# A convolution and a token mixer on one core: chunks enter the rounds three at a time, and the first step's sums lie in other buffers

## The chip, the cores and the metric

The kernel runs on one core of a Trainium2 chip. The metric is the device time of one execution in microseconds; the time before is the median of three runs.

## The reference

The input `x` is 8 x 4224 x 192 (batch, token, channel). A causal convolution with 7 taps per head runs over the tokens; the taps are a softmax of `weight`. Its result, again called `x`, goes through a phase mixer:

```
x     = conv(x, softmax(weight))              # 8 heads of 24 channels, 7 taps
theta = x @ w_theta                           # 192 x 192
zr, zi = x * cos(theta), x * sin(theta)
y     = w_tok_r @ zr + w_tok_i @ zi           # over the 4224 tokens, both matrices 4224 x 4224
u     = x + y
out   = u + relu(u @ w_ch)                    # 192 x 192
```

Nearly all of the arithmetic is the two token products.

## The kernel before

**Chunks, blocks and steps.** The 4224 tokens that are summed over are cut into 33 chunks of 128 (`NK`), the 4224 output tokens into 33 blocks of 128. Two blocks form a unit, so there are 17 units (`NU`), the last with one block only. A chunk is prepared once: its convolved `x`, its cosine and sine products and some differences of them lie in a tile `z` of seven fields. It then stays for 17 consecutive steps, and in each step it meets one unit. Eleven chunks (`NW`) fit at a time: the pool `zpool` has eleven slots. The list `base` says in which step of a round each of the eleven enters, and `start` extends it to three rounds of 18 steps; a slot so has one step between two chunks. A step `t` thus works on `n` chunks (2 to 11) and one unit. There are 58 steps.

**A step's products.** The four products of a two-block unit with real and imaginary weights are done with seven runs instead of eight (sums of weights and of `z` fields, as in Strassen's scheme). A run takes each of the `n` chunks in turn, with a pair of matmuls per chunk (`L405`, 128 x 384, two halves of the columns). A unit of one block takes four runs. The results stand in PSUM tiles `y`, two of them (`ypool`); `give` adds a finished one to the sums `pv` in SBUF on VectorE (`L370`), or, in the first 17 steps, copies some of them on ScalarE (`L368`). A tile `y` is used again only after the `give` that reads it. At the end of a step the sums go to `part` in device memory (`L418`) and come back 17 steps later (`L341`); in the last 17 steps they are final, `x` is added (`add_x`), and `outputs` casts, transposes, multiplies by `w_ch` and stores them.

**Weights.** For each step, pieces of the two token matrices are loaded by POOL's queue to `st` (`L295`), two steps ahead. VectorE turns them to `wt` (`L308`, four turns) and forms four sums of weights (`L320`), one step ahead.

**Chunks.** `load_chunk` loads a window of the input, `xw`, in four pieces by POOL's queue (`L183`); four halo pieces are copied from the window of the chunk before by SP's queue (`L174`). The preparation is a list of tasks: two `conv` (eight matmuls each at `L196`, copied out by ScalarE at `L148`; after the second, the convolved rows are stored to `xs`, `L213`), two `transpose` (`L153`), two `theta` (`L138`, with two sines on ScalarE at `L233`), two `product` (`L238`) and two `sums` (`L244`) on VectorE. All matmul results but `y` share a PSUM pool of two buffers (`mmpool`).

**Buffers.** Windows `xw` and sums `pv` share the tag `big` of the pool `wk`, with six slots.

**Order.** The helpers `pe`, `dve`, `act` and `pool` keep the written order on four engines (POOL's for weight loads and `add_x`, not for windows). Inside a step, work is put among the mix pairs at times counted in sevenths of the step: `step_events` gives a time to each task, `mix` carries it out when that point comes. The tasks of chunks that enter in the next step stand at 0.1 plus 0 to 3.6, and the next chunk's 2.3 later.

**The fill.** The first eleven chunks are prepared by the loop at `L611`, one conv-to-sums pipeline over 13 iterations. `between(n)` puts up to `n` mix pairs between the stages, as far as their chunk is `ready` (chunk `i-2` from the middle of iteration `i`); in the iterations 1 and 2 matmuls on a zero tile (`idle`, `L537`, here called noise) fill in.

Of the kernel before, what the change touches and what calls it, by code (L numbers as in the profile page):

```python
# [12 lines left out]
F32 = mybir.dt.float32  # L13
# [3 lines left out]
def kernel(  # L17
# [27 lines left out]
    P = nc.NUM_PARTITIONS  # L45
    assert (B, D, P) == (8, 192, 128) and S % P == 0
    N = B * D
# [13 lines left out]
    NW = 11  # L61
    PC = 512

    base = [0, 0, 1, 1, 2, 3, 3, 4, 4, 5, 5]
    assert len(base) == NW
    start = [base[k % NW] + (NU + 1) * (k // NW) for k in range(NK)]
    NSTEP = start[-1] + NU
# [26 lines left out]
    wk = ctx.enter_context(tc.tile_pool(name="wk", bufs=2))  # L94
    zpool = ctx.enter_context(tc.tile_pool(name="zpool", bufs=NW))
# [64 lines left out]
    Z11, T1, Z21, Z22, T2, T4, T3 = range(7)  # L160
# [102 lines left out]
    def load_chunk(k):  # L263
        if k < NK and k not in chunks:
            chunks[k] = Chunk(k, before=chunks[k - 1] if k % NW else None)
# [7 lines left out]
    class Step:  # L273
# [62 lines left out]

        def load_rows(self):
            for tb in self.tbs:
                pv = wk.tile([P, N], F32, name="pv", tag="big", bufs=6)
                if not self.first:  # L340
                    nc.sync.dma_start(  # L341
                        out=pv, in_=part[(self.t // NU - 1) % 2][tb, :, :]
                    )
                self.pv.append(pv)
# [122 lines left out]
    def step_events(t):  # L467
        found = []
        s = steps[t]
        if t + 1 < NSTEP:  # L470
            found += steps[t + 1].w_tasks()
            found.append((1.6, steps[t + 1].load_rows))
            if steps[t + 1].final and not steps[t + 1].ahead:
                for i in range(len(steps[t + 1].tbs)):
                    found.append((3.3 + 1.7 * i, lambda i=i: steps[t + 1].add_x(i)))
        for s in steps[t:]:
            if s.ahead and t == s.t - (4 if s.late else 10):
                for i in range(len(s.tbs)):
                    found.append((3.3 + 1.7 * i, lambda s=s, i=i: s.add_x(i)))
        if t + 2 < NSTEP:  # L480
            nxt = steps[t + 2]
            for m in (1, 2):
                found.append((1.3 + 3 * (m - 1), lambda m=m: nxt.load_w(m)))
        for at, f in outputs:
            begin = at - sum(s.time for s in steps[:t])
            if 0 <= begin < steps[t].time:
                found.append((7 * begin / steps[t].time, f))
        if t >= NU - 2:
            new = [k for k in range(NK) if start[k] == t + 2 and k >= NW]
            for k in new:  # L490
                found.append((4.5, lambda k=k: load_chunk(k)))
            at = 0.1
            for k in (k for k in range(NK) if start[k] == t + 1 and k >= NW):
                pos = [0, .5, 1.3, 1.6, 2.1, 2.5, 3.1, 3.15, 3.4, 3.6]

                def add(at, j, k):
                    def go():
                        if j == 0:
                            chunks[k].todo = chunks[k].tasks()
                        next(chunks[k].todo)()  # L500
                    found.append((at, go))
                for j, p in enumerate(pos):
                    add(at + p, j, k)
                at += 2.3
        return found


# [10 lines left out]
    for a in range(2):  # L518
        nc.gpsimd.affine_select(
            out=sel, in_=sel, pattern=[[1, Q - 1 + 2 * WR]], channel_multiplier=-1,  # L520
            base=-(Q - 1 + HALO - KS + 1 + a * WR), compare_op=ALU.not_equal, fill=1.0,
# [13 lines left out]
    def idle(n):  # L535
        for _ in range(n):
            pe(nc.tensor.matmul(  # L537
                spare[:, 0, 0:BH], lhsT=noise[:, 0:P], rhs=noise, start=True, stop=True
            ))
# [47 lines left out]
    def stream():  # L587
        for t in range(NSTEP):
            yield from steps[t].mix(step_events(t))
# [5 lines left out]
    def more(n):  # L595

        for i in range(n):
            if need[0] is None:
                need[0] = next(flow, NK)
            if need[0] > ready[0]:  # L600
                return n - i
            need[0] = next(flow, NK)
        return 0
# [7 lines left out]
    for i in range(NW + 2):  # L611
        ch = chunks.get(i) if i < NW else None
        old = chunks[i - 1] if 0 < i <= NW else None

        def between(n):
            left = more(n)
            if 0 < i < 3:
                idle(min(left, 2))

        if ch:  # L620
            ch.conv(0)
        between(3)
        if old:
            old.theta(0)
        between(2)
        if ch:
            ch.conv(1)
        if i == 0:
            idle(4)
        ready[0] = i - 2  # L630
        between(3)
        if old:
            old.theta(1)
        if i == 1:
            for _, f in steps[0].w_tasks():
                f()
        if i + 3 < NW:
            load_chunk(i + 3)
        between(2)
        if ch:  # L640
            ch.transpose(0)
        if old:
            old.product(Z11)
        between(1)
        if ch:
            ch.transpose(1)
        between(1)
        if old:
            old.product(Z21)
            old.sums(0)  # L650
            old.sums(1)
        between(2)
    nc.vector.memset(wch[:, 1:3, :], 0.0)
    for rows, i, part_w in channel_pieces(moe_w_ch):
        nc.gpsimd.dma_start(out=wch[rows, i, :], in_=part_w)
# [34 lines left out]
```

## Time and profile before

| what | value |
|---|---|
| median of 3 runs | 1474.13 us (1471.6 to 1476.81) |
| the profiled execution's own time | 1474.01 us |
| its span in the profile | 1472.3 us |
| TensorE (PE) busy | 1435.7 us, 10100 matmuls |
| VectorE (DVE), ScalarE (ACT) busy | 1001.1 us, 361.1 us |
| mix matmuls (L405) | 7656 |
| matmuls on the zero tile (L537) | 36 |
| stores of sums to `part`, loads back | 79 and 79, 768 KB each |
| windows of the input, pieces (L183) | 132 |

In the profile a row names line, engine and operation, then what is written and read, and how often. PE is the matmul, PEld the weight load, DVE is VectorE, ACT ScalarE, POOL GpSimd and SP SyncE. In a timeline a line begins with start and duration in us; brackets at the end hold the idle time of the engine before it and what ended it. Matmuls overlap, so the duration of one is longer than its distance to the next.

### The profile page before, as it was taken

What the parts mean: (1) busy time and instruction counts of PE and PEld (TensorE: products, weight loads), DVE (VectorE), ACT (ScalarE), POOL (GpSimd) and SP (SyncE); (2) the same over time, 40 slices, a digit from 0 to 9 for tenths busy, and PEclk for the clock granted to TensorE, in tenths of its full rate; (3) what the DMA queues carried; (4) which work ended last, traced back from release to release, by engine and by line L of the source; (5) the groups of instructions that cost most, each with busy time, mean ns of one, the idle gap of its engine ahead of it and who ended that gap; (6) DMA issues with size and microseconds to landing.
All of it is one profiled execution on the core that took longest, in us unless ns stands there. A gap on an engine that the chain in (4) does not pass through costs nothing.

```text
span 1472.3 us, 24451 instructions
## 1 busy us (share of the span) xinstructions
PE 1435.7 (98%) x10100; PEld 905.6 (62%) x10100; DVE 1001.1 (68%) x1050; ACT 361.1 (25%) x461; POOL 429.4 (29%) x659
## 2 busy tenths in 40 slices
PE   7899999999999999999999999999999999999997
PEld 5565666666666666566666656666666666666664
DVE  6784545454548687766666657778787778778585
ACT  5771111111134254000000005245122222222234
POOL 7422211121233232211112323332224243544220
PEclk9999999999999999999999999999999999999999
DMA  9986657465699999987779989999778777999873
GB/s 165 201 187 145 130 98 152 95 145 102 120 246 218 214 243 241 202 215 152 215 154 224 226 184 231 191 229 263 144 176 200 190 177 180 211 253 223 198 200 109
DMA packets 234975, 274.16 MB, mean 186 GB/s; under 512 B 69104, under 2 KB 202608, under 8 KB 234864
## 3 DMA queue, kind: packets, MB, share of 16 engines
q0 software_dynamic: 163616, 95.30, 49.1%
q1 hardware_dynamic: 71248, 177.30, 33.9%
q8 instruction: 79, 1.29, 0.3%
q14 instruction: 32, 0.26, 0.1%
HBM read 245.49 MB, written 111.28 MB: 242 GB/s over the span
## 4 chain that ended last, share of the span: by engine, by line
PE 87%; DMA 5%; DVE 4%; ACT 1%; issue 1%; SPq 0%; POOL 0%; DVEq 0%; ACTq 0%; POOLq 0%
PE y L405 78%; PE v L138 5%; PE tp L153 2%; PE pc L196 2%; DVE pv L370 1%; DVE wt L308 1%; DMA part<-pv 1%; DMA xw<-xw 1%; DMA st<-in_moe_w_tok_i_dram 1%; DVE z L244 1%; DMA xw<-in_x_dram 1%; ACT z L233 1%; DVE z L238 1%; DMA pv<-part 1%; DVE pv L434 0%
## 5 line engine op out<-in xcount | busy, mean ns | idle before, releaser
L405 PE MATMUL y<-z,wt 128*128 128x384 f16 x7656 | 1297.6, 326 | 12.4 <-DVE pv L370 11.6
L405 PEld LDWEIGHTS <-wt 128*128 128x128 f16 x7656 | 738.4, 98 | 481.6 <-issue 17.5
L370 DVE TENSOR_TENSOR pv<-y,pv 128x768 f32<-128x768 f32 x324 | 308.6, 953 | 376.2 <-PE y L405 362.9
L308 DVE STREAM_TRANSPOSE wt<-st 128x1408 f16<-128x1408 f16 (+7 forms) x224 | 326.5, 1463 | 4.8 <-DMA st<-in_moe_w_tok_i_dram 4.6
L295 POOL DMA_DIRECT2D st<-in_moe_w_tok_i_dram x232 | 132.5, 579 | 502.9 <-DVE wt L308 487.6
L295 POOL DMA_DIRECT2D st<-in_moe_w_tok_r_dram x232 | 132.5, 579 | 467.1 <-DVE wt L308 447.8
L320 DVE TENSOR_TENSOR wt<-wt 128x1408 f16<-128x1408 f16 (+7 forms) x216 | 204.0, 945 | 10.9 <-PE y L405 8.2
L148 ACT ACTIVATE uT<-tp 128x768 f16<-128x768 f16 x127 | 102.2, 814 | 294.9 <-PE tp L153 293.3
L148 ACT ACTIVATE z<-pc 128x768 f16<-128x768 f32 x65 | 52.9, 813 | 387.0 <-PE pc L196 387.0
L368 ACT ACTIVATE pv<-y 128x768 f32<-128x768 f32 x66 | 53.6, 815 | 280.1 <-PE y L405 279.8
L138 PEld LDWEIGHTS <-uT 128*128 128x128 f16 x1056 | 91.8, 98 | 24.0 <-issue 8.3
L434 DVE SCALAR_TENSOR_TENSOR pv<-v,pv 128x768 f32<-128x768 f32 x66 | 62.6, 950 | 44.3 <-PE v L138 42.1
L183 POOL DMA_DIRECT2D xw<-in_x_dram x132 | 76.1, 584 | 28.3 <-DMA st<-in_moe_w_tok_r_dram 9.8
L424 ACT ACTIVATE ub<-pv 128x768 f16<-128x768 f32 x66 | 54.8, 837 | 90.2 <-DVE pv L370 89.2
L244 DVE TENSOR_TENSOR z<-z 128x768 f16<-128x768 f16 x132 | 73.5, 557 | 4.2
L233 ACT ACTIVATE z<-v,half_pi 128x768 f16<-128x768 f32 x66 | 59.5, 902 | 45.9 <-PE v L138 45.9
L238 DVE TENSOR_TENSOR z<-z 128x1536 f16<-128x1536 f16 x66 | 60.6, 949 | 13.4 <-ACT z L233 13.4
L352 POOL TENSOR_TENSOR pv<-pv,xr 128x1536 f32<-128x1536 f32 x20 | 62.5, 3124 | 7.6 <-issue 6.9
L138 PE MATMUL v<-wch,uT 128*128 128x192 f16 x528 | 54.2, 246 | 3.9 <-DVE pv L434 2.2
L138 PE MATMUL v<-wth,uT 128*128 128x192 f16 x528 | 55.3, 248 | 1.4 <-ACT z L233 1.3
L233 ACT ACTIVATE z<-v 128x768 f16<-128x768 f32 x66 | 53.1, 805 | 0.0
L153 PE MATMUL tp<-ident,z 128*128 128x128 f16 x396 | 33.4, 222 | 6.3 <-ACT z L233 6.2
(43 smaller groups left out, 203.0 us busy)
## 6 DMA issues: line engine op xcount, KB each, us to landing
part<-pv SPq DMA_DIRECT2D x79, 768.0 KB, 4.1
pv<-part SPq DMA_DIRECT2D x79, 768.0 KB, 5.4
out_dram<-pv SPq DMA_DIRECT2D x66, 384.0 KB, 4.4
st<-in_moe_w_tok_r_dram POOLq DMA_DIRECT2D x136, 176.0 KB, 6.0
st<-in_moe_w_tok_i_dram POOLq DMA_DIRECT2D x136, 176.0 KB, 4.8
xs<-z SPq DMA_DIRECT2D x132, 96.0 KB, 4.3
xw<-in_x_dram POOLq DMA_DIRECT2D x121, 96.0 KB, 5.8
part<-xs POOLq DMA_DIRECT2D x26, 384.0 KB, 6.9
```

The costliest lines, as they stand in the source:

```text
L138: pe(nc.tensor.matmul(v[:, k, b * D : (b + 1) * D], lhsT=tT[:, 3 * k + b + i, :], rhs=w[:, 2 * b + i, :], start=(i == 0), stop=(i == 1),))
L148: act(nc.scalar.activation(out=out, in_=in_, func=AT.Copy))
L153: pe(nc.tensor.transpose(tp[:, 0, k * P : (k + 1) * P], u[:, k * P : (k + 1) * P], ident))
L183: nc.gpsimd.dma_start(out=self.xw[lo : lo + n, h, :, :], in_=x[:, t0 : t0 + n, :].rearrange("b s d -> s b d"),)
L233: act(nc.scalar.activation(**args))
L238: dve(nc.vector.tensor_tensor(out=o, in0=xv, in1=o, op=ALU.mult))
L244: dve(nc.vector.tensor_tensor(out=z[:, o, :], in0=z[:, a, :], in1=z[:, b, :], op=ALU.subtract))
L295: pool(nc.gpsimd.dma_start(out=st[a * Q : (a + 1) * Q, 0:nb, :, 0:n] .rearrange("i r bt s -> i (r bt) s"), in_=w[self.tbs[0] * P : (self.t ...
L308: dve(nc.vector.transpose(self.w[name][:, 0 : self.n, :, :], self.st[int(name[1])][:, int(name[0]) - 1, :, 0 : self.n * Q] .rearrange("p b ...
L320: dve(nc.vector.tensor_tensor(out=self.w[name][:, 0 : self.n, :, :], in0=self.w[a][:, 0 : self.n, :, :], in1=self.w[b][:, 0 : self.n, :, : ...
L370: dve(nc.vector.tensor_tensor(out=o, in0=yv, in1=o, op=ALU.add))
L405: pe(nc.tensor.matmul(y[cn][:, q, 0:BH], lhsT=self.w[wn][:, c, :, :].rearrange("p bt i -> p (bt i)"), rhs=chunks[k].z[:, zn, q * BH : (q + ...
```

## The change

Four things change. The list `base` lets three chunks enter per step instead of mostly two, which makes 56 steps of 58; the steps at the seams hold 3, 6, 9 and 8 chunks where they held 2, 4, 5, 7, 9 and 10, and the last steps 8, 5 and 2 where they held 9, 7, 6, 4 and 2. The sums of step 0 are taken from `zpool`, whose slots the later chunks use, and not from `big`. In later rounds the tasks of the next entering chunk start 1.6 instead of 2.3 after those of the one before. In the fill the calls of `between` allow 10 pairs an iteration instead of 14, and stand between the two `sums` too.

```diff
-    base = [0, 0, 1, 1, 2, 3, 3, 4, 4, 5, 5]
+    base = [0, 0, 0, 1, 1, 1, 2, 2, 2, 3, 3]
...
             for tb in self.tbs:
-                pv = wk.tile([P, N], F32, name="pv", tag="big", bufs=6)
+                if self.t == 0:
+                    pv = zpool.tile([P, N], F32, name="pv", tag="z")
+                else:
+                    pv = wk.tile([P, N], F32, name="pv", tag="big", bufs=6)
...
                 for j, p in enumerate(pos):
                     add(at + p, j, k)
-                at += 2.3
+                at += 1.6
...
         if ch:
             ch.conv(0)
-        between(3)
+        between(2)
         if old:
             old.theta(0)
-        between(2)
+        between(1)
         if ch:
             ch.conv(1)
         if i == 0:
             idle(4)
         ready[0] = i - 2
-        between(3)
+        between(2)
         if old:
             old.theta(1)
...
         if i + 3 < NW:
             load_chunk(i + 3)
-        between(2)
+        between(1)
         if ch:
             ch.transpose(0)
         if old:
@@
         between(1)
         if ch:
             ch.transpose(1)
+        if old:
+            old.product(Z21)
         between(1)
         if old:
-            old.product(Z21)
             old.sums(0)
+        between(1)
+        if old:
             old.sums(1)
-        between(2)
+        between(1)
```

## The prediction

> **What bounds the kernel now.** First the page: busy shares, the 40 slices, the chain that ended last, the costliest group.
>
> ```profile
> PE 1435.7 (98%) x10100; PEld 905.6 (62%) x10100; DVE 1001.1 (68%) x1050; ACT 361.1 (25%) x461; POOL 429.4 (29%) x659
> ...
> PE   7899999999999999999999999999999999999997
> ...
> PE 87%; DMA 5%; DVE 4%; ACT 1%; issue 1%; SPq 0%; POOL 0%; DVEq 0%; ACTq 0%; POOLq 0%
> ...
> L405 PE MATMUL y<-z,wt 128*128 128x384 f16 x7656 | 1297.6, 326 | 12.4 <-DVE pv L370 11.6
> ```
>
> TensorE is the bound: 98% busy, full in all slices but the first two and the last. The change keeps all 7656 mix matmuls and every chunk's own work, so it moves the time only through TensorE's idle time. Where is that? The stage table (us, then busy of PE, weight load, DVE, ACT, POOL; clock; DMA share; GB/s) and TensorE's timeline say:
>
> ```profile
> 50.80:92.62 41.82, 38.13 (x350) 25.07 (x350) 36.26 (x52) 36.12 (x49) 17.63 (x31) 1.00 1.13 234
> 92.62:113.04 20.42, 16.75 (x136) 11.16 (x136) 19.01 (x27) 12.22 (x16) 5.21 (x9) 0.98 0.60 116
> ...
> 453.80:480.50 26.70, 26.70 (x217) 17.16 (x216) 22.39 (x27) 12.68 (x16) 6.82 (x12) 1.00 1.03 249
> ```
> ```profile
> 42.40 0.80 PE L405 MATMUL y<-z,wt 128*128 128x384 f16 x2 [3.89 <-DVE pv L370]
> 42.99 1.48 PE L138 MATMUL v<-wth,uT 128*128 128x192 f16 x8
> ...
> 96.97 0.82 PE L138 MATMUL v<-wth,uT 128*128 128x192 f16 x8
> ...
> 99.48 0.49 PE L153 MATMUL tp<-ident,z 128*128 128x128 f16 x6 [0.38 <-ACT z L233]
> ...
> 113.04 12.18 PE L405 MATMUL y<-z,wt 128*128 128x384 f16 x66 [3.29 <-DVE pv L370]
> ```
>
> Idle sits in the fill (0 to 113 us, with two waits above 3 us for a sum, "give", that stood late in VectorE's queue) and in the tail after 1440. In the seams where later chunks enter (427 to 587, 878 to 1034) it is 0.73, 0.41, 0.73, 0.48 and 0.80: 3.15 us in all. A step there (third row) is full on TensorE, with VectorE at 22.4 of 26.7 us.
>
> **What the Trainium skill says.** "TensorE: Matmul & The Clock Gate" (Part 1) lets the clock fall to half after an idle window of about 3.4 us. The trace agrees: after 3.89 us idle, eight theta matmuls took 1.48 us, not 0.82; after 3.29 us, 66 mix matmuls took 12.18 us, not 66 x 0.163 = 10.8. The same page ("Architectural detail") calls DVE a strict FIFO; the late gives behave so. "DMA: Bandwidth & Descriptors" ("Issuing engines are not separate DMA queues") has SP's and POOL's transfers interleave on the same 16 engines. The DMA views of 460 to 467, and of 448 to 456 (last line), fit; KB each and median us to landing close each line:
>
> ```profile
> pv<-part SPq DMA_DIRECT2D x1, 768.0 KB, 9.1
> st<-in_moe_w_tok_r_dram POOLq DMA_DIRECT2D x4, 144.0 KB, 8.8
> xw<-in_x_dram POOLq DMA_DIRECT2D x4, 96.0 KB, 9.8
> ...
> part<-pv SPq DMA_DIRECT2D x2, 768.0 KB, 5.8
> ```
>
> Early in a step everything lands late: x pieces issued there took 7.1 to 10.7 us in six steps, against 5.0 to 5.7 elsewhere in these seams.
>
> **The fill.** A pair of mixes costs 0.326 us (the row's 326 ns is latency; 66 in 10.8 us gives 163 ns each). Before, 120 pairs (240 records at L405) were done by 113.04, and the cold clock then cost 1.4 us more: 114.4. After, counting the rounds' quotas against "ready": with three chunks in step 0 no pair beyond the second runs before chunk 2 is ready, so the iterations get 0, 0, 1, 1, 7, 10, 7, 7, 10, 10, 10, 10 pairs, 73 by the end of iteration 11. How long is an iteration? A chunk's matmuls take 2.88 us (conv 2 x 0.45, transposes 2 x 0.33, theta 2 x 0.66, by start-to-start). The PSUM pool of two makes the second theta, and the second transpose, wait for the two sines before it: the theta that ends near 97.63 releases the transpose at 99.48, 1.85 us later. Old cover: 0.65 + 0.45 + 0.98 = 2.08 us (no wait) and 0.65 + 0.33 + 0.33 = 1.31 (0.54 wait): 2.88 + 14 x 0.326 + 0.54 = 8.0; measured 8.27 (58.36 to 66.63). New cover: 0.33 + 0.45 + 0.65 = 1.43 (0.42 wait) and 0.33 + 0.33 + 0.33 = 0.99 (0.86 wait): 2.88 + 3.26 + 1.28 = 7.4, with the same excess 7.65. So 1.3 us of mixes left each iteration and it shortens by only 0.6. With conv(0) at 10.3, the first three as measured (4.4, 7.7, 6.7), then 6.7 (like the third, nothing to interleave), 6.9, 8.5 (0.8 for the frequent gives of step 0), 6.9, 7.6, 3 x 7.65 and 5.4 without a new chunk, iteration 11 ends at 94.1; 47 pairs more reach 120 at 109.4. Against 114.4 this is 5.0 us less: what comes back is the two long waits and their cold clock, since VectorE meets fewer small steps. Iteration 3 lacks both noise and mixes (about half busy); for a cold clock or a hiccup there I take off 1.5. **Gain 3.5**, from -1 to 8.
>
> The step-0 sums in z slots free two "big" slots, so windows of chunks 3 to 10 no longer wait for stores; POOL's queue was 8.3 us idle at 54.6 behind a weight turn, and after the first two no conv waited over 0.2 us. Nothing by itself; without it three-chunk steps would stall the fill. Five noise matmuls less: inside the waits, nothing.
>
> **Two steps fewer.** With each full step go 15 DVE tasks, two stores, two loads of sums and eight weight loads, none on TensorE's path in the steady stretch (VectorE 13.6 of 25.1 us there): nothing. In the tail, late steps of 8, 5 and 2 chunks replace 9, 7, 6, 4, 2; of the waits of 0.48, 0.46 and 0.36 at 1401 to 1449 half go. **Gain 0.7**, 0 to 1.5. The last step and its outputs are alike.
>
> **Three chunks enter in a step.** Steps 17 to 19 and 35 to 37 hold 8 chunks: 56 x 0.326 + 3 x 2.88 = 26.9 us of TensorE. VectorE: four turns at 1.23 and four sums at 0.68 (interpolated between the 7- and 9-chunk rows), seven gives at 0.87, three chunks at 4.05: 26 us, 97%. Following its queue, the third chunk's products fall between the step's last two gives; these still end 0.3 to 0.6 us before the bank is wanted. I take 1 us in all, 0 to 8.
>
> ACT's share: with pitch 1.6 a theta and the other chunk's conv come at one point; cover 0.45 + 3.2 pairs = 1.5 us against 1.85, once per chunk but the last: 0.4 a step with rounding, 2.4 in six. From 0 to 5.
>
> Now the buffers. "big" has six slots. A step takes five (two sums, three windows) where it took four. Laid out in the built order, the first two windows get slots of used windows or stored sums; the third gets that of the running step's first sum row. Its POOL load waits for that row's last give and for its store. In steps 18, 19, 36, 37, with the step starting at 0: the give ends at about -0.6, the store lands 5.8 later, 5.3; four POOL issues at 0.58, the last from 7.2; landing 8.5 (middle of 7.1 to 10.7): 15.7. The third conv stands at 3.3 of 7: 27 pairs, 8.8, plus 4.4 of chunk matmuls and 0.4 of waits: 13.6. TensorE is in order, so it idles 2.1 us, four times: 8.4. In steps 17 and 35 the give is 2 us earlier: 0.3 each. Sum **9.0**; from 0 (landing 6) to 20 (landing 10.7, store 7). Queued behind on POOL is the next weight load, wanted 20 us later: free. On SP the window's halo copies stand ahead of the second row's store and the xs stores; the first chunk's xs store then lands near 12, and the sums that overwrite its source come at 17: free.
>
> From this go about 2 of the 3.15 us of seam idle. Seams: 9.0 + 2.4 + 1 - 2 = +10.4. **Sum:** 10.4 - 3.5 - 0.7 = +6.2 on the profiled execution's 1474.0 (span 1472.3 and 1.7 around it; the median of three is 1474.1): 1480.2.
>
> **Rivals.**
> - In time: the third window lands by 13.6, because loads spread over three chunks meet an emptier queue (median in the whole seam is 6.0, and DMA share is not above 1.06). Then seams cost 1.4, and 1.4 - 4.2 gives 1471. The point is a landing of 6.4 us. Against: every early-step load was slower than that. This one is not slower.
> - The fill gives back all its waits (8) and the tail 1.5, with windows in time: 1474 + 1.4 - 9.5 = 1466. For: 7.2 us of the fill's waits are two single gives. Against: shorter covers in each iteration.
> - VectorE binds: at 97% a give misses its bank at each seam. The only overfull step of before (step 40, 21.7 us of DVE on 17.5 of TensorE) idled 0.48 + 0.80; six such seams add 7 to the forecast: 1487.
>
> **Chances.** About 0.3% (4.4 us) is what a measurement of this kernel can tell from no change. Forecast 0.42 and VectorE rival 0.15, both slower; in time 0.24, same; full fill 0.19, faster. The range goes from the full-fill case, 1466, to the forecast with windows at their upper price (11 more) and 3 us of the other ends, 1494; the slower cases alone span 1478.5 to 1494.
>
> **What would show it.** Right: conv matmuls (L196) in four of six three-chunk steps after a wait of 1 to 4 us; such steps near 30 us; iterations of about 7.6 us; no fill wait above 3 us; the 120th pair near 110. Wrong: those conv matmuls without a wait, x landing in 6 us, or a fill that ends later than before.

## The result and the profile after

| kernel | median us | ratio to before, 95% interval | span of the profiled execution |
|---|---|---|---|
| before | 1473.31 (4 runs) | | 1472.3 |
| after | 1488.45 (1488.04 to 1489.02, 4 runs) | 1.010 [1.008, 1.012] | 1486.3 |

The changed kernel is slower by 15 us, 1.0%. The forecast was 1480.2: the right side, but 8 us too low.

The page of the kernel after, its busy times, slices, chain and three groups (busy time and mean ns of one, then idle time of the engine just before them and what ended most of it):

```profile
PE 1438.6 (97%) x10095; PEld 907.5 (61%) x10095; DVE 993.2 (67%) x1020; ACT 359.7 (24%) x461; POOL 426.5 (29%) x639
...
PE   7899999999999979999999999989999999999997
...
PEclk9999999999999989999999999999999999999999
...
PE 86%; ACT 4%; DVE 3%; DMA 3%; issue 2%; SPq 1%; POOL 0%; DVEq 0%; ACTq 0%; POOLq 0%
...
L408 PE MATMUL y<-z,wt 128*128 128x384 f16 x7656 | 1291.7, 327 | 2.0 <-DVE pv L373 1.7
...
L183 POOL DMA_DIRECT2D xw<-in_x_dram x132 | 76.2, 584 | 76.2 <-DMA part<-pv 21.3
...
L196 PE MATMUL pc<-xw,bands 96*64 96x192 f16 x528 | 38.2, 262 | 17.2 <-DMA xw<-in_x_dram 14.1
```

Three things are to be seen. The mix matmuls, which waited 11.6 us for gives, now wait 1.7. In the fill (up to step 17) these waits fall from 8.4 us to under 0.4, while TensorE's waits for sines rise from 7.0 to 11.8 us; all its waits together fall from 21.4 to 18.2. The fill has lost its late gives, not its idle time. The convolutions at L196, which waited for no window before, now wait 14.1 us for windows of the input. And the slices of TensorE have two new dips, the 15th (520 to 557 us, with the clock down as well) and the 27th (966 to 1003): one in each seam.

TensorE's waits in the kernel after (total, times, longest) give the same two numbers:

```profile
PE pc L196 <- DMA xw<-in_x_dram: 14.1, 5, 6.6
...
PE y L408 <- DVE pv L373: 1.7, 5, 0.4
```

**How large is each part?** The two kernels enter chunks in different steps, so equal times do not mean equal work. Three marks in the trace divide the run: the first convolution of step 17, that of step 35, and the first transpose of the first final outputs. Counting the chunks of each step gives how many mix pairs more or fewer the kernel after does in each stretch; at 0.3257 us a pair (from long stretches of mixes) this is taken out. The marks, first before, then after:

```profile
427.07 0.52 PE L196 MATMUL pc<-xw,bands 96*64 96x192 f16 x8
877.43 0.52 PE L196 MATMUL pc<-xw,bands 96*64 96x192 f16 x8
1059.06 0.50 PE L153 MATMUL tp<-ident,ub 128*128 128x128 f16 x6
```
```profile
448.15 0.52 PE L196 MATMUL pc<-xw,bands 96*64 96x192 f16 x8
911.20 0.52 PE L196 MATMUL pc<-xw,bands 96*64 96x192 f16 x8
1053.88 0.50 PE L153 MATMUL tp<-ident,ub 128*128 128x128 f16 x6
```

| stretch | before, us | after, us | pairs more in after | change without them |
|---|---|---|---|---|
| fill, to step 17 | 427.07 | 448.15 | +91 (29.64 us) | -8.6 |
| first seam and the steps behind it | 450.36 | 463.05 | 0 | +12.7 |
| second seam, to the first outputs | 181.63 | 142.68 | -154 (50.16 us) | +11.2 |
| to the end of the span | 413.24 | 432.42 | +63 (20.52 us) | -1.3 |

The sum is +14.0, the difference of the spans. Of the fill's 8.6 us, 1.1 belong to this execution: the 32 tap matmuls at the start took 1.57 us where they took 2.64 in the profile before. So both parts of the forecast were too small: the fill gives 7.5 and not 3.5, the seams cost 24 and not 10. TensorE's waits in the two seams grow from 3.2 to 18.6 us, which is 15.4 of these 24; the other 8.5 are matmuls at a lowered clock behind the long waits and steps that are themselves longer, and were not divided further.

**The fill.** Two lines of TensorE's timeline (start and duration; in brackets the idle time before and what ended it):

```profile
85.01 0.49 PE L153 MATMUL tp<-ident,z 128*128 128x128 f16 x6 [0.70 <-ACT z L233]
...
89.26 22.91 PE L408 MATMUL y<-z,wt 128*128 128x384 f16 x140
```

The 0.70 for the sines of the chunk before is the most that one of the last four iterations waits (convolutions start 7.6 us apart: 63.73, 71.27, 78.87), and from 89.26 the mixes run without a gap. 136 mix matmuls, 68 pairs, were done by then; 52 more at 0.326 bring the 120th pair to 106.2. Before it was at 114.7: the prediction's 114.4 counts 240 mix matmuls by 113.04, and the trace has 238.

**The seams.** The stage table of the four steps from the first mark (stretch and length, then busy time of PE, weight load, DVE, ACT and POOL; clock, DMA share, GB/s):

```profile
448.15:476.36 28.21, 27.89 (x246) 18.55 (x245) 20.64 (x27) 19.25 (x25) 11.37 (x20) 1.00 1.04 211
476.36:504.97 28.61, 28.11 (x246) 18.59 (x245) 24.83 (x34) 18.79 (x24) 9.15 (x17) 1.00 1.18 260
504.97:534.41 29.44, 28.34 (x245) 18.77 (x244) 25.39 (x34) 18.68 (x24) 11.17 (x20) 1.00 1.04 231
```
```profile
534.41:563.00 28.59, 21.29 (x163) 13.75 (x163) 12.05 (x17) 10.88 (x14) 4.56 (x8) 0.82 0.78 201
```

The first three are the steps in which three chunks are prepared. They are nearly full on TensorE; only the third has a visible gap. The great gap lies in the step behind them, in which only two chunks are prepared. TensorE's timeline, first one line from step 18, 14.1 us after its start at 476.36, then the gap:

```profile
490.48 0.52 PE L196 MATMUL pc<-xw,bands 96*64 96x192 f16 x8
```
```profile
547.76 0.34 PE L196 MATMUL pc<-xw,bands 96*64 96x192 f16 x1 [6.62 <-DMA xw<-in_x_dram]
548.78 0.85 PE L196 MATMUL pc<-xw,bands 96*64 96x192 f16 x7 [0.68 <-DMA xw<-in_x_dram]
549.56 2.74 PE L408 MATMUL y<-z,wt 128*128 128x384 f16 x8
552.10 1.49 PE L138 MATMUL v<-wth,uT 128*128 128x192 f16 x8
```

The first line is the convolution of a *third* window: no bracket, no wait. None of the six third windows was late. The window that is late is the *second* of its group, by 6.62 + 0.68 us; after this stretch the clock is down: from the eight mix matmuls to the next line it is 2.54 us (at full clock 8 x 0.163 = 1.3), and the theta takes 1.49 instead of 0.82. In the second seam the same happens to the second window of step 37, with 3.83 and 2.16 us. Why is it late? POOL's timeline, on which the windows (L183) are issued:

```profile
529.25 0.59 POOL L183 DMA_DIRECT2D xw<-in_x_dram  x1
539.86 0.58 POOL L295 DMA_DIRECT2D st<-in_moe_w_tok_r_dram  x1 [10.02 <-DVE wt L308]
540.66 2.28 POOL L183 DMA_DIRECT2D xw<-in_x_dram  x4 [0.22 <-issue]
```

and VectorE's:

```profile
536.87 1.14 DVE L244 TENSOR_TENSOR z<-z 128x768 f16<-128x768 f16 x2
537.93 1.64 DVE L308 STREAM_TRANSPOSE wt<-st 128x1408 f16<-128x1408 f16 x1
```

Between the group's first window and its second stands a piece of the weights for a later step. In the text of the kernel this piece comes after both windows, but the helper `pool` does not hold windows to the written order, and in the queue as built the piece is ahead. It may be loaded only when VectorE has turned the weights that lie in its buffer, and this turn stands in VectorE's queue behind the last sums of the third chunk of the step before. So POOL stands still for 10.02 us, and the window behind it cannot go.

For part of this time it could not have gone anyway. In the kernel as built its buffer is that of the third window of the group before, from which SP first has to copy the halo of the next window; and these copies stood on SP behind eight stores of convolved rows:

```profile
519.00 9.18 SPq L213 DMA_DIRECT2D xs<-z  x8
528.29 2.71 SPq L174 DMA_DIRECT2D xw<-xw  x4
...
534.04 2.58 SPq L174 DMA_DIRECT2D xw<-xw  x4
```

The four copies at 528.29 landed 3.4 to 4.2 us after their issue. At 534.04 SP could already write the late window's own halo into that buffer. So it was free by then, and the weight piece held the window for 6.6 us more. Its four pieces start at 540.66, 6.2 us into the step; TensorE wants them at 547.76 - 6.62 = 541.1, and they took 6.4 us (median of the four) to land. In the second seam POOL waited 9.18 us at the same place.

### The profile page after: what moved, and what is told of

It is laid out like the page before. It is cut to its first block, busy times and chain, and to the rows that moved or that the text cites. A ratio compares the mean times of both kernels' runs of the same rounds, so it can differ in the third digit from the quotient of the medians.

```text
span 1486.3 us, 24378 instructions
## 1 busy us (share of the span) xinstructions
PE 1438.6 (97%) x10095; PEld 907.5 (61%) x10095; DVE 993.2 (67%) x1020; ACT 359.7 (24%) x461; POOL 426.5 (29%) x639
## 4 chain that ended last, share of the span: by engine, by line
PE 86%; ACT 4%; DVE 3%; DMA 3%; issue 2%; SPq 1%; POOL 0%; DVEq 0%; ACTq 0%; POOLq 0%
PE y L408 78%; PE v L138 5%; ACT z L233 3%; PE tp L153 2%; PE pc L196 1%; DMA xw<-in_x_dram 1%; DMA xw<-xw 1%; DVE pv L373 1%; DVE z L244 1%; ACT uT L148 1%; DVE wt L320 0%; DVE wt L308 0%; DMA st<-in_moe_w_tok_i_dram 0%; SPq L174 0%; DVE z L238 0%
## 5 line engine op out<-in xcount | busy, mean ns | idle before, releaser
L373 DVE TENSOR_TENSOR pv<-y,pv 128x768 f32<-128x768 f32 x310 | 295.4, 953 | 407.0 <-PE y L408 394.1
L308 DVE STREAM_TRANSPOSE wt<-st 128x1408 f16<-128x1408 f16 (+5 forms) x216 | 325.0, 1510 | 0.3 <-DMA st<-in_moe_w_tok_i_dram 0.3
L295 POOL DMA_DIRECT2D st<-in_moe_w_tok_i_dram x224 | 128.0, 579 | 494.5 <-DVE wt L308 488.0
L295 POOL DMA_DIRECT2D st<-in_moe_w_tok_r_dram x224 | 127.9, 579 | 433.7 <-DVE wt L308 429.9
L320 DVE TENSOR_TENSOR wt<-wt 128x1408 f16<-128x1408 f16 (+5 forms) x208 | 208.9, 1004 | 11.0 <-PE y L408 8.3
L138 PEld LDWEIGHTS <-uT 128*128 128x128 f16 x1056 | 91.9, 98 | 30.0 <-issue 15.4
L183 POOL DMA_DIRECT2D xw<-in_x_dram x132 | 76.2, 584 | 76.2 <-DMA part<-pv 21.3
L355 POOL TENSOR_TENSOR pv<-pv,xr 128x1536 f32<-128x1536 f32 x24 | 75.5, 3144 | 11.6 <-ACT ub L427 5.3
L196 PE MATMUL pc<-xw,bands 96*64 96x192 f16 x528 | 38.2, 262 | 17.2 <-DMA xw<-in_x_dram 14.1
```

Of the source, the lines that this page charges most:

```text
L138: pe(nc.tensor.matmul(v[:, k, b * D : (b + 1) * D], lhsT=tT[:, 3 * k + b + i, :], rhs=w[:, 2 * b + i, :], start=(i == 0), stop=(i == 1),))
L183: nc.gpsimd.dma_start(out=self.xw[lo : lo + n, h, :, :], in_=x[:, t0 : t0 + n, :].rearrange("b s d -> s b d"),)
L295: pool(nc.gpsimd.dma_start(out=st[a * Q : (a + 1) * Q, 0:nb, :, 0:n] .rearrange("i r bt s -> i (r bt) s"), in_=w[self.tbs[0] * P : (self.t ...
L308: dve(nc.vector.transpose(self.w[name][:, 0 : self.n, :, :], self.st[int(name[1])][:, int(name[0]) - 1, :, 0 : self.n * Q] .rearrange("p b ...
L320: dve(nc.vector.tensor_tensor(out=self.w[name][:, 0 : self.n, :, :], in0=self.w[a][:, 0 : self.n, :, :], in1=self.w[b][:, 0 : self.n, :, : ...
L355: pool(nc.gpsimd.tensor_tensor(out=self.pv[i], in0=self.pv[i], in1=xr, op=ALU.add))
```

## The experiments

Each ratio is to the kernel before, run on the same chip beside it; the before kernel's medians there were 1473.9 to 1474.1.

**1. The windows ahead of the weights.** Kernel after, with the later windows' loads in POOL's written order, the first two ahead of the second weight load.

```diff
-                nc.gpsimd.dma_start(
+                load = nc.gpsimd.dma_start(
...
+                if k >= NW:
+                    pool(load)
...
-            for k in new:
-                found.append((4.5, lambda k=k: load_chunk(k)))
+            for j, k in enumerate(new):
+                found.append((4.25 if j < 2 else 4.6, lambda k=k: load_chunk(k)))
```

> The changed kernel, with POOL's queue order written out where later chunks enter: the first two windows of a group are loaded ahead of the imaginary weights of their step (at 4.25 instead of 4.5), the third behind them (4.6), and none behind the weight load of the next step. Slots, steps and all arithmetic are those of the changed kernel (1488.5 us, span 1486.3). Theory Q (the windows of steps 20 and 37 stood in POOL's queue behind a weight load that waited for a VectorE turn): the waits of 7.3 and 6.0 us before L196 in these steps fall under 2 us, with the cold clock after the first of them some 15 us go, 1473 to 1477 us. Theory V (VectorE at 97% is late with everything, the weight turn too): the windows come earlier, but as much time is lost on late turns and gives, 1484 to 1488. Theory T (the prediction's: the third window, in the slot of the running step's sums, sets the wait): nothing changes, since that slot is the same, 1488.

Measured: 1478.62 us (1477.79 to 1480.11), ratio 1.0032 [1.0020, 1.0044]: 9.8 us faster than after, on the same fill. By the marks the seams now cost 7.0 and 7.0 us instead of 12.7 and 11.2. POOL in that kernel, in the same place, and TensorE's first convolution of that step and those of the second window:

```profile
535.80 2.29 POOL L183 DMA_DIRECT2D xw<-in_x_dram  x4 [12.07 <-PE y L410]
538.08 2.16 POOL L297 DMA_DIRECT2D st<-in_moe_w_tok_i_dram  x4
```
```profile
538.62 0.52 PE L198 MATMUL pc<-xw,bands 96*64 96x192 f16 x8
...
546.11 0.24 PE L198 MATMUL pc<-xw,bands 96*64 96x192 f16 x1 [0.76 <-DMA xw<-xw]
546.95 0.49 PE L198 MATMUL pc<-xw,bands 96*64 96x192 f16 x7 [0.60 <-DMA xw<-xw]
```

The second window now starts 2.8 us ahead of its step (535.80 against 538.62) and not 6.2 us into it. POOL still stands for 12.07 us before it, but now for the window's own buffer: the halo copies that read from it landed at 535.1 (they are what its load waits for in the kernel as built; the bracket names a matmul that ended after them). TensorE's two long waits are gone. What is left in TensorE's waits are windows and halo copies that come a little late, 0.3 to 1.7 us at a time:

```profile
PE pc L198 <- DMA xw<-xw: 4.6, 7, 0.9
...
PE pc L198 <- DMA xw<-in_x_dram: 1.7, 1, 1.7
```

The weight load ahead of the window is so shown to cost 9.8 us, two thirds of the net loss; theory Q had hoped for 11.5 to 15.5. The edit fixes the order of all three windows of a group; the third was late in neither kernel.

**2. Fourteen pairs between the stages again.** Kernel after with the calls of `between` of before.

```diff
-        between(2)
+        between(3)
         if old:
             old.theta(0)
-        between(1)
+        between(2)
...
```

> The changed kernel with the old calls of between in the fill (14 pairs an iteration, both sums after one call). The fill of the changed kernel reached the same work 8.6 us sooner than before. Theory C (a pair between the stages is free as long as it covers a wait for the sines, so more pairs lose less): about 4 pairs more in each of 6 iterations for 0.6 us each, 3 to 5 us faster than the changed kernel, 1484. Theory G (the gain came from fewer gives in VectorE's queue per iteration): the long give waits of before come back in part, 3 to 8 us slower, 1492 to 1496.

Measured: 1492.85 us, ratio 1.0132 [1.0114, 1.0151], 4.4 us slower than after. The fill's gain at the first mark falls to 4.8 (from 7.5, since this execution had the 2.64 us start of before), and waits for gives of 1.06 and 1.55 us are back at 48 and 106 us. Fewer pairs are worth some 4 us of the median; in these two profiles 2.7 us of it stand in the fill.

**3. Entry as before.** Kernel after with `base` and pitch of before; z slots and ten pairs kept.

```diff
-    base = [0, 0, 0, 1, 1, 1, 2, 2, 2, 3, 3]
+    base = [0, 0, 1, 1, 2, 3, 3, 4, 4, 5, 5]
...
-                at += 1.6
+                at += 2.3
```

> The changed kernel with the old entry list and pitch (0,0,1,1,2,3,3,4,4,5,5 and 2.3): 58 steps, seams as before, but step 0's sums in z slots and 10 pairs an iteration in the fill. If the seams alone made the change slower (12.8 and 11.2 us by the traces) and the fill's 8.6 us come from the fewer pairs and the z slots, 1465 us. If they come from the wider first steps (three chunks in step 0, fewer gives), the fill is as slow as before or slower by the shorter covers (0.7 us in each of 8 iterations): 1473 to 1479 us.

Measured: 1470.79 us (1468.81 to 1471.84), ratio 0.9977 [0.9969, 0.9985]: faster than before. The seams cost next to nothing (450.36 and 181.63 us before, 449.80 and 182.43 here), and of the fill's gain 3.7 us remain (with the start of before). All of the loss comes with the entry in threes and its pitch. The pitch was not tried apart: at 2.3 the last task of a third chunk would stand at 0.1 + 4.6 + 3.6 = 8.3 sevenths, beyond the end of the step. The time lies between the two expectations, since the fill keeps half of its gain and not all or none of it.

**4. The first step's sums back in "big".**

```diff
-                if self.t == 0:
-                    pv = zpool.tile([P, N], F32, name="pv", tag="z")
-                else:
-                    pv = wk.tile([P, N], F32, name="pv", tag="big", bufs=6)
+                pv = wk.tile([P, N], F32, name="pv", tag="big", bufs=6)
```

> The changed kernel with step 0's sums back in the six big slots. The prediction held that windows of the fill would then wait for the stores of step 0: two windows later by some 5 us each, the fill 3 to 8 us longer, 1492 to 1496 us. Rival: the windows are loaded so far ahead that nothing waits, 1488 us.

Measured: 1488.04 us, ratio 1.0100 [1.0081, 1.0118], the same as after. The first mark stands at 449.05 against 448.15, and this execution had the 2.64 us start. The z slots neither bring nor prevent anything that shows here.

**5. The windows earlier still.** As 1, but in seam steps the first two windows at 1.7 and the next sums' loads at 3.0 instead of 1.6.

```diff
-            found.append((1.6, steps[t + 1].load_rows))
+            seam = any(start[k] == t + 2 for k in range(NW, NK))
+            found.append((3.0 if seam else 1.6, steps[t + 1].load_rows))
...
+                found.append((1.7 if j < 2 else 4.6, lambda k=k: load_chunk(k)))
```

> As the run with the windows first, but the first two windows of a group are loaded still earlier (at 1.7 of the step before, pinned behind the first weight load), the next step's sums after them (3.0 instead of 1.6 where windows are on their way) and the third window at 4.6, so that the second window gets a slot that is free early. In the run before (1478.6 us, seams 7.0 us longer than in the kernel before the change, each) the second window still waited 0.4 to 1.7 us, mostly for halo copies into a slot that a third window had just left. Theory Q (late windows, whatever makes them late, are the seam's loss): 5 to 7 us more go, 1472 to 1474 us, and no wait over 0.5 us stands before the second window's conv. Theory W (what is left is TensorE's own excess per three-chunk step, 1.3 us against 0.4): the waits go, but the time only to 1475 to 1477 us. Theory V (VectorE at 97%): gives become late instead, 1478 or more.

Measured: 1478.86 us (1475.45 to 1481.20), ratio 1.0034 [1.0025, 1.0043]: no better than 1. The profiled execution was its shortest, 1475.45. In its seams TensorE waits for no window at all; instead it waits for gives. VectorE, TensorE and SP there:

```profile
505.57 1.15 DVE L246 TENSOR_TENSOR z<-z 128x768 f16<-128x768 f16 x2 [3.88 <-DMA xs<-z]
506.64 0.95 DVE L375 TENSOR_TENSOR pv<-y,pv 128x768 f32<-128x768 f32 x1
```
```profile
507.64 0.48 PE L410 MATMUL y<-z,wt 128*128 128x384 f16 x2 [2.78 <-DVE pv L375]
```
```profile
489.14 9.27 SPq L174 DMA_DIRECT2D xw<-xw  x8
498.51 1.94 SPq L215 DMA_DIRECT2D xs<-z  x4
```

Read from the bottom: eight halo copies of the earlier windows hold SP's queue for 9.27 us (4.2 of them a pause between the first four and the other four, which need a window that lands at 495.7), so the store of the third chunk's rows is issued late; the sums that overwrite these rows wait 3.88 us for it on VectorE; the give behind them is late, and TensorE idles 2.78 us. In the second seam waits for gives of 1.25 and 2.50 us stand at the like places. One wait has taken the place of another.

**6 and 7. The second theta and what follows later in the sequence**, once on top of 5, once alone on after.

```diff
-                pos = [0, .5, 1.3, 1.6, 2.1, 2.5, 3.1, 3.15, 3.4, 3.6]
+                pos = [0, .5, 1.3, 1.6, 2.1, 2.65, 3.25, 3.3, 3.5, 3.6]
```

> As the run with early windows, and the second theta of a chunk stands 0.55 of a run after the first (was 0.4), its products 0.6 after it, the last sums at 3.6 as before. Theory W: the cover of the two sines grows from 0.45 + 3 to 4 pairs (1.4 to 1.7 us) to 0.45 + 4 to 5 pairs (1.8 to 2.1 us) against the 1.85 us that they take; the waits of 0.33 us before the second theta go, twice in each of six steps: 3 to 4 us faster than the run with early windows. Rival: products and sums closer together (VectorE's last burst) make the gives at the step's end late, same or slower.

> The changed kernel with only the wider spacing of the two thetas. By theory W 3 to 4 us faster than the changed kernel (1488.5), 1485, since the windows wait as before; if the window waits absorb it (a step that is shorter meets the same window later), 1488.

Measured: on top of 5, 1476.90 us, ratio 1.0020 [1.0012, 1.0027], 2 us better, at the edge of what these runs can tell (the intervals of 5 and 6 overlap). Alone, 1493.73, ratio 1.0133 [1.0117, 1.0148], 5 us *worse* than after, which neither expectation allowed. In both, the theta's short waits for sines fall from 5.7 us (22 times) to 3.0 and 3.4; alone, the waits for halo copies grow from 0.8 to 3.9 us and the longest for a window from 6.6 to 7.7. By the marks 2.6 of the 5 us lie in the seams; the others fall behind them, and no wait in the trace accounts for these.

**8. Only fewer pairs.** Kernel before with the new calls of `between` and nothing else.

```diff
-        between(3)
+        between(2)
         if old:
             old.theta(0)
-        between(2)
+        between(1)
...
```

> The kernel before with only the new calls of between (10 pairs, sums apart): old entry list, old pitch, step 0's sums in big. With the sums in z slots this took 1470.8 us, 3.3 us less than before. If the fewer pairs alone bring that, 1471; if the z slots are needed for it (the window of chunk 8 waits for the store of step 0), 1474 to 1477.

Measured: 1469.79 us (1467.23 to 1471.45), ratio 0.9972 [0.9964, 0.9980]. This is the fastest kernel of the study and beats both: 4 us less than before, 19 less than after. At the first mark it is 4.75 us ahead of before, 1.1 of this by the faster start, and the seams are as before (449.79 and 181.62 us). TensorE's waits for gives have shrunk from 11.6 us, not gone:

```profile
PE y L405 <- DVE pv L370: 6.5, 8, 1.8
```

**9. Threes in the fill, the old order in the seams.** Kernel after with two lists: the new `base` for the first eleven chunks, the old one (and 2.3) for the others.

```diff
-    base = [0, 0, 0, 1, 1, 1, 2, 2, 2, 3, 3]
+    base = [0, 0, 1, 1, 2, 3, 3, 4, 4, 5, 5]
...
+    wide = [0, 0, 0, 1, 1, 1, 2, 2, 2, 3, 3]
-    start = [base[k % NW] + (NU + 1) * (k // NW) for k in range(NK)]
+    start = [(base if k >= NW else wide)[k % NW] + (NU + 1) * (k // NW) for k in range(NK)]
...
-                at += 1.6
+                at += 2.3
```

> Edit: the first eleven chunks enter as in the kernel after (base of after, sums of step 0 in z slots, 10 pairs an iteration), the 22 later chunks as in the kernel before (its base, pitch 2.3; 58 steps). Theory (the fill and the seams are separate parts whose gains and losses add): the fill's gain of 8.6 us stays, seams and tail are as before, so 1474.0 - 8.6 = 1465.4, some 4 us faster than the version with fewer pairs alone (1469.8); the seams show no wait of TensorE for a window. Rival (the entry in threes pays in the fill only because the seams then stand elsewhere; or step 0 and 1 with six chunks have their own cost later): 1469 to 1472.

Measured: 1492.43 us, ratio 1.0123 [1.0107, 1.0139]: a miss by 27 us. The fill's gain is there (first mark 449.06: 7.7 us after the 91 pairs), the second seam costs nothing (181.63 us), but the first takes 445.42 us where 450.36 - 29.64 = 420.7 were due: +24.7. The expectation forgot that chunks leave as they came, 17 steps later. They leave in threes and are replaced in twos and ones, so steps 17 to 22 hold 8, 7, 6, 5, 7 and 9 chunks where the kernel before holds 9 or 10. Short steps carry the same gives, sums' loads and stores as long ones. The stage table around the shortest:

```profile
511.00:523.00 12.00, 6.13 (x27) 3.04 (x26) 7.13 (x10) 0.00 (x0) 6.26 (x11) 0.86 0.98 157
523.00:550.00 27.00, 20.66 (x156) 12.67 (x157) 17.55 (x24) 12.46 (x16) 9.10 (x16) 0.87 1.00 205
```

TensorE is half idle in the first row, VectorE is not full either, DMA share is at 1: waits for gives (1.2 and 2.8 us), for a window (2.81) and, as the profile puts it, for a halo copy (2.54) follow each other, and the clock falls to 0.87. Which of these would go if another were removed was not tried.

**10 and 11. The row stores on ScalarE's queue.** Kernels 5 and 1, with the stores to `xs` of chunks 11 to 32 issued from ScalarE instead of SP.

```diff
-                    nc.sync.dma_start(
+                    (nc.scalar if self.k >= NW else nc.sync).dma_start(
                         out=xs[t0 : t0 + Q, :], in_=self.x[a * Q : (a + 1) * Q, :]
```

> Edit: the early-window version (windows pinned, the first two at 1.7, next sums at 3.0), with the stores of the convolved rows of chunks 11 to 32 issued from ScalarE's queue and not from SP's. There the sums task of the third chunk waited for that store on VectorE (3.88 and 4.60 us), behind halo copies on SP (9.27 us for eight), and the give behind it made TensorE idle 2.78, 1.25 and 2.50 us. Theory S (SP's order makes the gives late): those give waits go, 6 us, 1478.9 - 6 = 1473. Rival V (VectorE is simply full in these steps): the same gives are late by as much, 1477 to 1480. Rival A (issuing on ScalarE delays sines and conv copies, each 0.8 to 0.9 us long there): the waits for sines grow, 1479 or more.

> Edit: the windows-first version (windows pinned in POOL's order, 4.25 and 4.6), with the stores of the convolved rows of chunks 11 to 32 issued from ScalarE's queue and not from SP's. There TensorE still idled 7.3 us for halo copies and windows in the seams (waits of 0.3 to 1.7 us, mostly xw from xw). Theory S (halo copies come late because they stand on SP behind eight stores of convolved rows, 9.88 us): these waits shrink to under 2 us, 1478.6 - 5 = 1473.5. Rival W (the halo copies wait for the window of the chunk before, which POOL issues late): the waits stay, 1477 to 1480. Rival A (ScalarE's own work is delayed): 1480 or more, with longer waits for sines.

Measured: 1503.49 us, ratio 1.0205 [1.0186, 1.0224], and 1518.20, ratio 1.0300 [1.0278, 1.0322]: 25 and 40 us slower than 5 and 1. The waits under test nevertheless go as the theory has it: in 10, VectorE's waits of 3.88 and 4.60 us for the store are gone and TensorE's for gives fall from 7.8 to 0.7 us; in 11, those for halo copies fall from 4.6 to 1.2. (The steps are longer here, which also leaves a late give or copy more time.) But TensorE's wait for sines rises to

```profile
PE tp L153 <- ACT z L235: 29.8, 24, 2.5
```

from 8.9 us, and in 11 from 8.6 to 39.3. ScalarE's timeline in 10 shows it:

```profile
494.28 3.11 ACTq L215 DMA_DIRECT2D xs<-z  x4
497.44 0.90 ACT L235 ACTIVATE z<-v,half_pi 128x768 f16<-128x768 f32 x1 [3.19 <-DMA xw<-xw]
```

The four stores stand on ScalarE for 3.1 us, and a sine for which TensorE waits stands behind them. Of the 3.1 us their issues take 1.84 (0.31 to 0.72 each); before the last of them ScalarE waits until a halo copy has landed, as the bracket says. "DMA: Bandwidth & Descriptors" of the Trainium skill ("Issuing engines are not separate DMA queues") says that initiating DMAs on several engines saves only the sequencer's time, usually small against the transfer. Here the four issues take 1.4 to 3.9 us in the 22 chunks of experiment 10, against a landing of 4.7 (median): smaller than the transfer, but not small, and taken from an engine on the path. The longer waits for sines are 20.9 us in 10 and 30.7 in 11; the rest of the 25 and 40 us was not traced.

## Why the prediction was wrong

**Right:** the bound (TensorE, though not through its idle time alone: of the seams' 24 us, 15.4 are waits), the side, and that the loss stands at L196 in waits for windows. This last is luck: the 9.0 us were worked out for the third windows, and not one of the 14.1 us measured at L196 stands there. The z slots bring nothing by themselves (experiment 4). Iterations of the fill take 7.6 us (7.65 forecast), no fill wait exceeds 3 us, and the two long gives and their cold clock are gone. The tail gave 1.3 us for 0.7.

**The third window, +9.0: measured 0.** This step failed. The working had the third window's load wait for the store of the running step's first sums, issue 5.3 to 7.2 us into the step and land 8.5 us later, at 15.7. The buffer and the store it waits for are as worked out, the sizes are not. In step 18 the load was issued 3.3 us into the step:

```profile
479.71 2.28 POOL L183 DMA_DIRECT2D xw<-in_x_dram  x4 [3.33 <-DVE z L244]
```

Its pieces landed in 3.4 to 4.0 us, 9 us into the step, and the convolution at 490.48 did not wait. Nor did any other third window; their pieces took 3.4 to 6.0 us. So the condition of the rival "In time" (a landing within 6.4 us) held, and the kernel lost all the same, since that rival too looked at third windows only.

The 8.5 us came from too narrow a reading of before. In its seams eight windows took 7.1 to 10.7 us with all four pieces, issued 5.0 to 8.8 us into their steps; the pieces of the others took 3.0 to 8.1, not 5.0 to 5.7. In the seams of after, the pieces issued next behind two loads of sums on SP (five windows, as at 490.89 behind 488.47) landed in 8.9 to 10.9 us and all others in 2.9 to 6.8. The third windows were never among the five. That the loads of sums are the cause was not tested.

**"Queued behind on POOL is the next weight load, wanted 20 us later: free."** This is the step that should have found the cost. It asked what stands behind the windows, not what stands ahead of them. Ahead of a second window (that of step 20, and that of step 37) stood a weight load that waits for VectorE, and the turn it waits for stood behind the sums of a third chunk. It held the first of them for 6.6 us after its buffer was free. Price: 7.3 us of TensorE (6.62 + 0.68) and 6.0 (3.83 + 2.16), with the cold clock behind it; taking it away returned 9.8 us (experiment 1). That a load on an in-order queue is as late as the latest of its predecessors was used for TensorE and VectorE and not for POOL.

**Thetas and steps, +2.4: more.** Two theta waits of 0.16 us a step show as brackets, 2 us in six steps, but the three-chunk steps take 28.2 us where 26.9 was computed from pairs and chunk work, before any window is late. The steps of before with two chunks take 26.7 where the same sum gives 26.3. So 1.3 us a step against 0.4, some 5 us in six steps over what the old seams have. The share of sines in this can be named only in part: with most theta waits gone (experiment 6) 2 us came back.

**VectorE at 97%: not reached.** The rows above have 20.6, 24.8 and 25.4 us of 28 to 29. It did not bind as such; it mattered by its order. The rival with full gives at each seam appeared only in experiment 5, for another reason: not the work but a store on SP in front of it. The prediction had called the like of this free for the first chunk's store ("the sums that overwrite its source come at 17"); for the third chunk's, with early windows, it was not.

**The fill, -3.5: measured -8.6.** The terms that were off: the 1.5 us set aside for a cold clock in iteration 3 was not needed; nor was the 0.8 for frequent gives in the sixth iteration (the convolution of chunk 6 stood 7.6 us after that of chunk 5, not 8.5); from the last chunk's convolution (78.87) on, the fill took 1.0 us less than worked out, five pairs set aside; and 1.1 us is the faster start of this execution. These are some 4.4 of the 5.1. Experiments 2 and 8 try the two parts of the other 7.5 alone: fewer pairs give 3.7, entry in threes 4.8. Together they would make 8.5, so the two overlap by 1 us. Less waiting is only 3.3 us of the gain; the cold clock behind the long gives is part of the rest, which was not divided.

**"Without it three-chunk steps would stall the fill" (the z slots): wrong**, by experiment 4.

**What stays open.** With the long window waits gone the entry in threes still costs 14 us by the marks in experiment 1 (7.0 in each seam), and 3.7 and 7.8 in the shortest execution of experiment 5. Late halo copies, late row stores, sines and the 1 us a step are parts of it; no run had all of them away at once, so whether the entry in threes could win with other queues was not shown.

## What to carry to other kernels

Before a load is called hidden, list what stands *ahead* of it on the queue that issues it, and for each of these what it waits for: a window was held for 6.6 us after its buffer was free, by a weight load that waited for VectorE. Then ask the same of its buffer: here halo copies behind stores on SP were the next wait in the row. Look also whether the kernel's text fixes that order at all; here it did not. When chunks enter faster in one part of a cyclic schedule, ask what this makes of the place where they leave (experiment 9 lost 25 us there). And try the parts alone: of four changes one, the number of pairs between stages, was worth 4 us, one was worth nothing, and the entry in threes took four times as much away.

## What was not expected of the hardware

Four 96 KB stores issued from ScalarE stood on it for 1.7 to 4.0 us (22 times in experiment 10), 1.4 to 3.9 of them for the issues alone. And the first 32 tap matmuls took 1.57 us in four of the thirteen profiles and 2.64 or 2.65 in the other nine, though the kernels have the same text up to there, so a difference of 1 us at the start of two profiles says nothing about an edit.
